# Longer runs for two weight loads, and the column order that goes with them

## The chip, the cores and the metric

The kernel runs on one core of a Trainium2 chip. The metric is the device time of one execution, in microseconds (us). The engines of a core work side by side, each from its own list of instructions: TensorE (PE; its weight loads are shown as PEld), VectorE (DVE), ScalarE (ACT), GpSimd (POOL) and SyncE (SP), which here does nothing but issue the transfers from device memory (DMAs). They wait for each other by semaphores.

## The reference, cut to what matters

One token per sequence, 8 sequences (B), model width 512 (D). First attention with 32 query heads over 8 key and value heads of a cache of which the last 2048 positions count, then a feed-forward block:

```python
x = A_x                                            # 8 x 512
h = x + A(_layernorm(x))                           # A: q = x@wq, softmax over 2048 keys, o, then o @ wo
u = _layernorm(h)                                  # what the block B gets
x1 = u + 0                                         # B's token shift is empty for one token, so w1, w2 add nothing
h2 = h + x1 + _gelu(_layernorm(x1) @ w3) @ w4      # w3: 512 x 1792, w4: 1792 x 512
```

All arrays are bf16. The keys and values that are read take 67 MB, wq and wo 4 MB each, w3 and w4 1.8 MB each.

## The kernel before, in words

**The stream.** SP issues all loads in one order written out by hand: wq, then 2 MB tiles of keys (`load_k`) and values (`load_v`) in turn, wo in three pieces (`load_wo`, heads 0 to 8, 8 to 24, 24 to 32 of each partition's 32 rows), then w3 (`load_w3`, 1792 KB) and w4 in three pieces (`load_w4`, 1024, 512 and 256 KB). All are recorded on one line, L207, in a helper `dma`, so they are told apart by the tile they write. The profile writes `w_sb` for both `w3_sb` and `w4_sb`. Each partition's share of a key tile is one run of 16 KB in device memory; w3 is loaded as four runs of 3584 bytes per partition (rows p, 128+p, 256+p, 384+p for partition p), w4's first piece (eight chunks of 128 rows) as two runs of four rows, 4096 bytes each.

**The attention** works through 64 tiles: PE turns a key tile (L383), ACT and DVE copy it out of PSUM (L393, L395), PE multiplies it with the queries (L408); softmax on DVE and ACT; then PE multiplies with the values (L504).

**The tail**, all on the last token of the chain and in this order on PE:

- `pe_x` (L565) starts the sum for h, kept with features on partitions: `hT_ps[:, nb*B:(nb+1)*B]` holds 128 features for 8 sequences, nb = 0 to 3. x is the stationary operand (the one that a weight load, LDWEIGHTS, puts into the array).
- `pe_wo_row` (L553) multiplies the first 20 of wo's 32 parts in row form, `pe_wo` (L574) the last 12 in column form: for each part and each nb, 128 columns of wo are loaded as the stationary operand and 8 columns of `oW` stream through. That makes 48 loads and 48 matmuls. `pe_hr` (L583, 8 loads) turns the row form over and adds it.
- mean, variance and normalisation: DVE L649 to L658, L689, L693, PE L652 and L683, ACT L692. `uT` (L654) is the normalised input of w3.
- `pe_w3` (L678): 14 column groups `fc`, 4 loads each of a 128 x 128 block of w3 as the stationary operand, 56 in all. Which columns belong to group fc is chosen by `w3_cols` so that the result lies as w4's rows do: with a run of k rows per partition, the columns are taken with a step of k. Before, W4_RUN is (4, 4, 4, 2): a step of four for groups 0 to 11, of two for 12 and 13.
- L703 on DVE scales, L705 on ACT applies gelu, in two halves, and L710 to L714 on DVE prepare the rest of the sum.
- `pe_w4` (L732): for each fc four matmuls side by side in four column strips of the array, each with `gT[:, fc, :]` stationary and 128 columns of w4 as the moving operand (the one that streams through). It comes in three calls, one for each piece of w4; `pe_fin` (L722) and a filler stand between the first two.
- L743 on ACT and L745 on DVE copy two strips each into `out_sb`, and SP stores it (L790).

Between these stand `warm_end(n)` calls (L493): n filler matmuls of 128x512 that nothing reads.

Of the kernel before, what the change touches and what calls it, by code (L numbers as in the profile page):

```python
# [11 lines left out]
B = 8  # L12
# [10 lines left out]
FC = F // 128  # L23
FG = FC // 2
KC = D // 128
# [54 lines left out]
def bass_sequential_preLN__sliding_block_cached__mixer_s_mlp__decode_kernel(  # L80
# [23 lines left out]
    with es:  # L104
# [13 lines left out]
        wo_v = wbig[:, :].rearrange("p (j n) -> p j n", j=JW)  # L118
        knat = sb([128, NK, CQ * DH], dt.bfloat16, "knat")
        vnat = sb([128, NV, CQ * DH], dt.bfloat16, "vnat")  # L120
        w3_sb = sb([128, KC, F], dt.bfloat16, "w3_sb")
        w4_sb = sb([128, FC, D], dt.bfloat16, "w4_sb")
# [13 lines left out]
        x_sb = sb([B, D], dt.bfloat16, "x_sb")  # L136
# [29 lines left out]
        sel32 = sb([128, H], dt.bfloat16, "sel32")  # L166

        orow = sb([128, 2, 512], dt.bfloat16, "orow")
        hr = orow
# [16 lines left out]
        out_sb = orow[0:B, 0, :]  # L186
# [13 lines left out]
        sem_x, sem_wq, sem_w3, sem_out = (S(n) for n in ("sem_x", "sem_wq", "sem_w3", "sem_out"))  # L200
        sem_wo = [S(f"sem_wo{i}") for i in range(len(WO_AT) - 1)]
        sem_w4 = [S(f"sem_w4{i}") for i in range(3)]
        PE, AC, DV, PO, SP = (Engine(S(n)) for n in ("s_pe", "s_act", "s_dve", "s_pool", "s_sp"))

        def dma(eng, dst, src, sem, *waits):
            def f(e):
                e.dma_start(dst, src).then_inc(sem, 16)  # L207
            eng.op(f, *waits, inc=False)
# [20 lines left out]
        e = DV.op(lambda e: e.bn_stats(st6[:, :], x_sb[:, :]), X)  # L229
        e = DV.op(lambda e: e.bn_aggr(mv[:, :], st6[:, :]), e)  # L230
        e = PO.op(lambda e: e.tensor_scalar(rstd[:, :], mv[:, 1:2], EPS, None, ALU.add), e)
        e = PO.op(lambda e: e.tensor_tensor(rstd[:, :], rstd[:, :], half[0:B, 0:1], ALU.pow), e)
# [8 lines left out]
        e = DV.op(lambda e: e.tensor_reduce(hsq[:, :], ident_f[:, :].rearrange("p (u h) -> p h u", u=4), AX.X, ALU.add))  # L241
# [7 lines left out]
        e = DV.op(lambda e: e.tensor_reduce(rows16[:, :].rearrange("p (t r) -> p t r", t=KQ),  # L249
                                            rows_f[:, :].rearrange("p (t s r) -> p t r s", t=KQ, s=NS), AX.X, ALU.add))  # L250
# [12 lines left out]
        e = PE.op(pe_xT, e_xln, e_idb)  # L263
# [67 lines left out]
        def q_turn():  # L331
            e_qT = []
            for j in range(2):
                def f(e, j=j):
                    for r in range(R):
                        ins = e.matmul(qT_ps[j][:, r * 128:(r + 1) * 128],
                                       qrow2[:, j, r, :, :].rearrange("p c d -> p (c d)").bitcast(dt.float32), ident_f[:, :],
                                       start=True, stop=True, is_transpose=True)
                    return ins
                e = PE.op(f, e_qrow[j], e_idf)  # L340
                got = qT_ps[j][:, :].bitcast(dt.bfloat16).rearrange("p (r u x) -> p r u x", r=R, u=4)[:, :, :, 0:2 * B]
                e_qT.append(DV.op(lambda e, j=j, got=got: e.tensor_copy(
                    qT[:, 4 * j:4 * (j + 1), :, :, :].rearrange("p u r b e -> p r u (b e)"), got), e))
            return e_qT[-1], e
# [145 lines left out]
        def warm_end(count):  # L490
            def f(e):
                for n in range(count):
                    ins = e.matmul(kbank[1], ident_b[:, :], still, start=True, stop=True)  # L493
                return ins
            PE.op(f, e_pT[LAST, 1])
# [49 lines left out]
        hT_ps = S_ps[0]  # L545
# [16 lines left out]
        def pe_x():  # L562
            def f(e):
                for nb in range(KC):
                    ins = e.matmul(hT_ps[:, nb * B:(nb + 1) * B], x_sb[:, nb * 128:(nb + 1) * 128],  # L565
                                   ident_b[0:B, 0:B], start=(nb == 0), stop=False, skip_group_check=True)
                return ins
            PE.op(f, free[0], X, e_idb)

        def pe_wo(j0, j1, piece):  # L570
            def f(e):
                for j in range(j0, j1):
                    for nb in range(KC):
                        ins = e.matmul(hT_ps[:, nb * B:(nb + 1) * B], wo_v[:, j, nb * 128:(nb + 1) * 128],  # L574
                                       oW[:, j, 0:B], start=False, stop=False, skip_group_check=True)
                return ins
            PE.op(f, (sem_wo[piece], 16))

        def pe_hr():
            def f(e):  # L580
                for part in range(2):
                    for nb in range(KC):
                        ins = e.matmul(hT_ps[:, nb * B:(nb + 1) * B], hr[:, part, nb * 128:(nb + 1) * 128], sel32[:, 0:B],  # L583
                                       start=False, stop=(part == 1), skip_group_check=True)
                return ins
            e_wo.append(PE.op(f, e_wo[-1], e_selb))
# [20 lines left out]
        e_qT, e_qturn = q_turn()  # L607
# [37 lines left out]
        def bc(a):  # L645
            return bass.AP(tensor=a.tensor, offset=a.offset, ap=[a.ap[0], [0, KC], [1, B]])


        e = DV.op(lambda e: e.tensor_reduce(hsum[:, :], vr(hT_ps[:, 0:NH]), AX.X, ALU.add), e_wo[-1])  # L649
# [11 lines left out]
        y_ps = [kbank[0], kbank[2]]  # L661
        FH = FC // 2

        W4_RUN = (4, 4, 4, 2)

        def w3_cols(kc, fc):
            at = 0
            for run in W4_RUN:
                if fc < at + run:
# [22 lines left out]
        e = AC.op(lambda e: e.activation(s2[:, :], vsum[:, :], ACT.Sqrt, bias=eps2[:, :], scale=1.0), e_vs)  # L692
        e_r2 = DV.op(lambda e: e.reciprocal(r2[:, :], s2[:, :]), e)  # L693

        def bcf(t):
            a = t[:, :]
            return bass.AP(tensor=a.tensor, offset=a.offset, ap=[a.ap[0], [0, FH], [1, B]])
# [3 lines left out]
        for n in range(2):  # L701
            cs = slice(n * FH * B, (n + 1) * FH * B)
            e = DV.op(lambda e, n=n, cs=cs: e.tensor_tensor(v3(g_x[:, cs]), v3(y_ps[n][:, 0:FH * B]), bcf(r2),  # L703
                                                            ALU.mult), e_y[n], e_r2)
# [3 lines left out]
        e = PO.op(lambda e: e.tensor_scalar(r1[:, :], vsum[:, :], EPS * (1.0 + EPS), None, ALU.add), e_vs)  # L708
        e = PO.op(lambda e: e.tensor_tensor(r1[:, :], r1[:, :], half[:, :], ALU.pow), e)
        e = DV.op(lambda e: e.tensor_tensor(v3(xb[:, :]), v3(hc[:, :]), bc(r1[:, :]), ALU.mult), e)  # L710
# [5 lines left out]
        z_ps = S_ps[1][:, 0:DH]  # L716

        def pe_fin():
            def f(e):
                for part in range(2):  # L720
                    for nb in range(KC):
                        ins = e.matmul(z_ps[32 * nb:32 * (nb + 1), :], fr[:, part, nb, :], ident_b[:, :],  # L722
                                       start=False, stop=False, tile_position=(0, 32 * nb), skip_group_check=True)
                return ins
            PE.op(f, e_fr)
        W4_AT = (0, 8, 12, FC)
        for n, waits in enumerate(((*e_gT, free[1]), (), ())):
            lo, hi = W4_AT[n:n + 2]
            def pe_w4(e, lo=lo, hi=hi):
                for fc in range(lo, hi):  # L730
                    for nb in range(KC):
                        ins = e.matmul(z_ps[32 * nb:32 * (nb + 1), :], gT[:, fc, :],  # L732
                                       w4_sb[:, fc, nb * 128:(nb + 1) * 128], start=(fc == 0), stop=(fc == FC - 1),
                                       tile_position=(0, 32 * nb), skip_group_check=True)
                return ins
            if n == 1:
                pe_fin()
                warm_end(1)
            e_z = PE.op(pe_w4, (sem_w4[n], 16), *waits)
        for nb in range(KC):  # L740
            to, got = out_sb[:, nb * 128:(nb + 1) * 128], z_ps[32 * nb:32 * nb + B, :]
            if nb % 2:
                e_outa = AC.op(lambda e, to=to, got=got: e.activation(to, got, ACT.Copy), e_z)  # L743
            else:
                e_outd = DV.op(lambda e, to=to, got=got: e.tensor_copy(to, got), e_z)  # L745
# [21 lines left out]
                            ap=[[KC * H * DH, k], [KC * k * H * DH, 4], [1, QF]]), sem_wf, e_wz if n else None)  # L767

        def load_w3():
            dma(SP, w3_sb[:, :, :], B_w3.rearrange("(k p) f -> p k f", p=128), sem_w3, e_qturn)  # L770

        def load_w4(n):
            lo, hi = W4_AT[n:n + 2]
            k = W4_RUN[-1] if hi == FC else W4_RUN[0]
            dma(SP, w4_sb[:, lo:hi, :].rearrange("p (g k) n -> p g (k n)", k=k),
                B_w4[lo * 128:hi * 128, :].rearrange("(g p k) n -> p g (k n)", p=128, k=k), sem_w4[n])

        turn = {"K": 0, "V": 0, "O": 0}
        for kind in "QKKK" + 9 * "VK" + "VKKVKVKVVVOVOO":
# [3 lines left out]
            {"K": load_k, "V": load_v, "O": load_wo}[kind](turn[kind])  # L783
            turn[kind] += 1
        load_w3()
        for n in range(3):
            load_w4(n)
# [39 lines left out]
```

## Time and profile before

| | us |
|---|---|
| median of 3 runs (192.92 to 194.08) | 193.04 |
| the profiled execution's own time | 193.02 |
| its span, first to last instruction | 191.6 |
| busy PE / PEld / DVE / ACT / POOL | 153.1 / 94.7 / 116.5 / 95.6 / 13.7 |

The span leaves out 1.42 us around the profiled execution, so a change in the span is added to 193.02. The page read 79.18 MB from device memory at a mean of 413 GB/s over the span; from the second slice of the page to the last but one the 16 DMA engines are busy without a gap. The granted TensorE clock is full (1.00) in all of the last 20 us. In the views, PE and PEld are two rows of one engine: loads run ahead of matmuls that are still streaming.

### The profile page before, as it was taken

How to read it: one execution, taken by the hardware profiler on the slowest of the kernel's cores; microseconds unless marked ns; L12 is line 12 of the kernel's file. 1: busy time of each engine (PE TensorE's matmuls, PEld its weight loads, DVE VectorE, ACT ScalarE, POOL GpSimd, SP SyncE). 2: the span in 40 equal slices, each digit the busy share in tenths (PEclk: the TensorE clock that was granted, in tenths of full speed). 3: DMA queues.
4: the chain of work that ended last, by engine and by line, in shares of the span. 5: the costliest groups of instructions: out<-in, count | busy, mean ns of one | idle time of the engine just before them, and what ended most of it. 6: DMA issues, size and time to landing. Idle time of an engine off the chain costs nothing.

```text
span 191.6 us, 3183 instructions
## 1 busy us (share of the span) xinstructions
PE 153.1 (80%) x1326; PEld 94.7 (49%) x1333; DVE 116.5 (61%) x259; ACT 95.6 (50%) x124; POOL 13.7 (7%) x37
## 2 busy tenths in 40 slices
PE   0049999598988988699978887889798895797895
PEld 0013866375556554465555455545554562343552
DVE  2733455834499368655885587558855886657423
ACT  3002667638357727284469255924782676340341
POOL 8400200100010001000100010002000000000040
PEclk9999999957999999789999999999999999699999
DMA  6999999999999999999999999999999999999991
GB/s 224 452 400 431 434 414 434 438 429 431 428 424 434 424 434 434 433 421 431 431 434 421 434 434 434 424 431 428 429 428 431 438 424 431 428 431 415 413 406 74
DMA packets 6477, 79.38 MB, mean 414 GB/s; under 512 B 688, under 2 KB 704, under 8 KB 1856
## 3 DMA queue, kind: packets, MB, share of 16 engines
q1 hardware_dynamic: 6448, 79.18, 97.3%
q8 instruction: 10, 0.16, 0.3%
q14 instruction: 3, 0.02, 0.0%
q10 hardware_dynamic: 16, 0.01, 0.0%
HBM read 79.18 MB, written 0.01 MB: 413 GB/s over the span
## 4 chain that ended last, share of the span: by engine, by line
DMA 55%; PE 20%; SPq 8%; DVE 8%; ACT 6%; issue 1%
DMA knat<-in_A_k_cache_dram 29%; DMA vnat<-in_A_v_cache_dram 11%; DMA w_sb<-in_B_w_dram 10%; SPq L207 8%; PE kT_ps L383 8%; DMA wbig<-in_A_wq_dram 6%; ACT kT_sb L393 3%; ACT pT_sb L472 3%; PE o_rows L504 3%; PE S_ps L504 3%; DVE kT_sb L395 2%; PE S_ps L302 2%; DVE oacc L516 2%; PE S_ps L408 2%; DVE omask L514 1%
## 5 line engine op out<-in xcount | busy, mean ns | idle before, releaser
L393 ACT ACTIVATE kT_sb<-kT_ps 128x1024 bf16<-128x1024 bf16 x64 | 65.6, 1025 | 54.9 <-PE kT_ps L383 54.7
L383 PE MATMUL kT_ps<-turn_f,knat 128*128 128x128 f32 x512 | 77.1, 291 | 13.8 <-DMA knat<-in_A_k_cache_dram 8.7
L383 PEld LDWEIGHTS kT_ps<-turn_f,knat 128*128 128x128 f32 x512 | 59.5, 147 | 35.0 <-issue 13.0
L395 DVE COPY kT_sb<-kT_ps 128x1024 bf16<-128x1024 bf16 x64 | 43.8, 685 | 25.4 <-PE kT_ps L383 25.2
L408 PE MATMUL S_ps<-kT_sb,qblk 128*32 128x512 bf16 x256 | 26.1, 401 | 2.7 <-ACT kT_sb L393 1.0
L504 PE MATMUL o_rows<-vnat,pT_sb 128*64 128x512 bf16 x128 | 16.5, 402 | 4.9 <-ACT pT_sb L472 4.9
L472 ACT ACTIVATE pT_sb<-o_rows,own_f 128x512 bf16<-128x512 f32 x28 | 17.7, 693 | 1.6 <-PE S_ps L408 1.2
L516 DVE TENSOR_REDUCE oacc<-omask 128x128 f32<-128x512 f32 x14 | 14.9, 1064 | 0.5
L504 PE MATMUL S_ps<-vnat,pT_sb 128*64 128x512 bf16 x112 | 13.4, 382 | 0.8 <-DMA vnat<-in_A_v_cache_dram 0.8
L504 PEld LDWEIGHTS o_rows<-vnat,pT_sb 128*64 128x64 bf16 x128 | 8.4, 114 | 11.3 <-issue 7.7
L350 POOL COPY qblk<-qT 64x64 bf16<-64x64 bf16 x16 | 5.0, 311 | 119.4 <-PE S_ps L408 106.4
L408 PEld LDWEIGHTS S_ps<-kT_sb,qblk 128*32 128x32 bf16 x256 | 6.6, 93 | 11.7 <-issue 6.9
L514 DVE TENSOR_TENSOR omask<-o_rows,own_s 128x512 f32<-128x512 f32 x7 | 4.8, 692 | 12.2 <-PE o_rows L504 12.2
L514 DVE TENSOR_TENSOR omask<-S_ps,own_s 128x512 f32<-128x512 f32 x7 | 4.8, 692 | 8.8 <-PE S_ps L504 8.8
L504 PEld LDWEIGHTS S_ps<-vnat,pT_sb 128*64 128x64 bf16 x112 | 5.8, 110 | 7.3 <-issue 2.0
L440 ACT ACTIVATE E_sb<-S_ps,negM 128x512 f32<-128x512 f32 x8 | 5.5, 689 | 6.5 <-DVE negM L436 6.5
L323 ACT ACTIVATE w_sb<-S_ps 128x512 bf16<-128x512 f32 x2 | 1.1, 594 | 11.4 <-PE S_ps L302 11.4
L259 PE MATMUL sm<-ident_b,xln_b 8*128 8x8 bf16 x4 | 0.3, 174 | 8.0 <-DVE xln_b L234 8.0
L529 PE MATMUL sm<-oacc,sel_o 128*128 128x256 f32 x16 | 6.1, 466 | 0.6 <-DVE oX L536 0.6
L431 DVE TENSOR_REDUCE mblk<-S_ps 128x1 f32<-128x512 f32 x8 | 5.5, 682 | 0.8 <-PE S_ps L408 0.8
L559 ACT ACTIVATE orow<-kT_ps 128x512 bf16<-128x512 f32 x1 | 0.6, 597 | 10.3 <-PE kT_ps L553 10.3
L453 DVE STREAM_TRANSPOSE PT_sb<-P_sb 128x512 bf16<-128x512 bf16 x8 | 5.6, 703 | 0.0
(118 smaller groups left out, 102.2 us busy)
## 6 DMA issues: line engine op xcount, KB each, us to landing
knat<-in_A_k_cache_dram SPq DMA_DIRECT2D x16, 2048.0 KB, 18.4
vnat<-in_A_v_cache_dram SPq DMA_DIRECT2D x15, 2048.0 KB, 20.1
wbig<-in_A_wq_dram SPq DMA_DIRECT2D x1, 3808.0 KB, 11.6
wbig<-in_A_wo_dram SPq DMA_DIRECT2D x2, 1024.0 KB, 22.5
knat<-in_A_v_cache_dram SPq DMA_DIRECT2D x1, 2048.0 KB, 19.8
wbig<-in_A_wo_dram SPq DMA_DIRECT2D x1, 2048.0 KB, 24.0
w_sb<-in_B_w_dram SPq DMA_DIRECT2D x1, 1792.0 KB, 29.9
w_sb<-in_B_w_dram SPq DMA_DIRECT2D x1, 1024.0 KB, 31.9
```

The lines of the kernel that those rows point to most:

```text
L207: e.dma_start(dst, src).then_inc(sem, 16)
L383: ins = e.matmul(kT_ps[i % 2][:, n * 256:(n + 1) * 256].bitcast(dt.float32), knat[:, j % NK, c * DH:(c + 2) * DH].bitcast(dt.float32), tur ...
L393: e_lo[i] = AC.op(lambda e: e.activation(kT_sb[:, i % NKT, 0:W // 2], kT_ps[i % 2][:, 0:W // 2], ACT.Copy), e_Tlo[i], e_QK.get(i - NKT))
L395: e_hi[i] = DV.op(lambda e: e.tensor_copy(kT_sb[:, i % NKT, W // 2:W], kT_ps[i % 2][:, W // 2:W]), e_Thi[i], e_QK.get(i - NKT))
L408: ins = e.matmul(S_ps[b % 2][32 * t:32 * (t + 1), :], qblk[:, b % 2, KQ * q + t, half, at:at + H], kT[:, :, t, :, half], start=(q == 0 and ...
L431: e = DV.op(lambda e: e.tensor_reduce(mblk[:, 0:1], S_ps[b % 2][:, :], AX.X, ALU.max), e_QK[G * b + G - 1], e_mz)
L453: e_PT[b] = DV.op(lambda e: e.transpose(PT_sb[:, :], P_sb[:, :]), e_P[b], e_wide.get(b - 1))
L472: e_pT[b, t] = AC.op(lambda e: e.activation(pT_sb[:, b % 2, :, H * t:H * (t + 1)], bank[:, :].rearrange("p (n y) -> p n y", n=NN), ACT.Cop ...
L504: ins = e.matmul(bank[64 * u:64 * (u + 1), :], pT_sb[:, b % 2, n, :].rearrange("p (x q) -> p q x", q=NQ)[:, q, :], v_tile(m)[:, n * 512:(n ...
L514: free[at] = DV.op(lambda e: e.tensor_tensor(omask[:, :, :], bank.rearrange("p (s d) -> p s d", s=NS), own, ALU.mult), e_PV[m], e_acc.get( ...
L516: e_acc[m] = DV.op(lambda e: e.tensor_reduce(acc, omask[:, :, :].rearrange("p s d -> p d s"), AX.X, ALU.add), free[at], e_O.get(b - 2))
L529: e_O[b] = PE.op(lambda e: e.matmul(O_ps, sel_o[:, :], oacc[:, b % 2, :, :].rearrange("p q d -> p (q d)"), start=True, stop=True), e_acc[N ...
```

## The change

Three edits that belong together. w3's rows are laid on the partitions in another order: partition p now gets rows 4p to 4p+3, one run of 14,336 bytes. The features of the normalised input must lie in the same order, so whatever writes them takes every fourth column, starting from nb, instead of a block of 128: x in `pe_x`, wo in `pe_wo`, the turned rows in `pe_hr`. Because the rest of the sum (`fin`) has the same order, w4's output columns and the place in `out_sb` get the step of four too. And w4's first piece is loaded with eight rows (8192 bytes) in one run, which makes `w3_cols` step by eight for groups 0 to 7; groups 8 to 11 keep four, 12 and 13 two.

```diff
         def pe_x():
-                    ins = e.matmul(hT_ps[:, nb * B:(nb + 1) * B], x_sb[:, nb * 128:(nb + 1) * 128],
+                    ins = e.matmul(hT_ps[:, nb * B:(nb + 1) * B], x_sb[:, nb::KC],
...
         def pe_wo(j0, j1, piece):
-                        ins = e.matmul(hT_ps[:, nb * B:(nb + 1) * B], wo_v[:, j, nb * 128:(nb + 1) * 128],
+                        ins = e.matmul(hT_ps[:, nb * B:(nb + 1) * B], wo_v[:, j, nb::KC],
...
         def pe_hr():
-                        ins = e.matmul(hT_ps[:, nb * B:(nb + 1) * B], hr[:, part, nb * 128:(nb + 1) * 128], sel32[:, 0:B],
+                        ins = e.matmul(hT_ps[:, nb * B:(nb + 1) * B], hr[:, part, nb::KC], sel32[:, 0:B],
...
-        W4_RUN = (4, 4, 4, 2)
+        W4_RUN = (8, 4, 2)
...
             def pe_w4(e, lo=lo, hi=hi):
-                                       w4_sb[:, fc, nb * 128:(nb + 1) * 128], start=(fc == 0), stop=(fc == FC - 1),
+                                       w4_sb[:, fc, nb::KC], start=(fc == 0), stop=(fc == FC - 1),
...
         for nb in range(KC):
-            to, got = out_sb[:, nb * 128:(nb + 1) * 128], z_ps[32 * nb:32 * nb + B, :]
+            to, got = out_sb[:, nb::KC], z_ps[32 * nb:32 * nb + B, :]
...
         def load_w3():
-            dma(SP, w3_sb[:, :, :], B_w3.rearrange("(k p) f -> p k f", p=128), sem_w3, e_qturn)
+            dma(SP, w3_sb[:, :, :].rearrange("p k f -> p (k f)"), B_w3.rearrange("(p k) f -> p (k f)", k=KC), sem_w3, e_qturn)

         def load_w4(n):
-            k = W4_RUN[-1] if hi == FC else W4_RUN[0]
+            k = W4_RUN[n]
```

The number and the order of instructions on every engine stay the same; on SP two of the 39 entries have another shape, w3's load and the first of w4's.

## The prediction

> **What bounds the kernel now.** I began with the page's strip of 40 slices: the DMA row stands at 9 from the second slice to the last but one, so the stream of loads sets the pace until close to the end. Then I read the end of the chain of work that ended last (start, duration, what):
>
> ```profile
> 170.00 19.17 DMA w_sb<-in_B_w_dram
> 189.17 0.04 issue
> 189.22 0.32 PE S_ps L732 x8
> ...
> 189.88 0.28 DVE orow L745
> ```
>
> The last thing waited for is w4's third piece, landed at 189.17; the last 8 matmuls, the copies and the store follow. To gain, that landing must come earlier; to lose, PE must become later than it. How close is PE? The timeline of the tail, PE's rows (start, duration, what, in brackets the idle time before):
>
> ```profile
> 180.15 1.27 PEld L574 LDWEIGHTS S_ps<-oW,wbig 128*128 128x128 bf16 x48 [0.42 <-issue]
> ...
> 181.65 0.27 PEld L583 LDWEIGHTS S_ps<-sel,orow 128*128 128x128 bf16 x8 [0.23 <-DVE orow L560]
> ...
> 183.53 1.24 PE L493 MATMUL kT_ps<-ident_f,ident_b 128*128 128x512 bf16 x5
> ...
> 184.93 1.87 PEld L678 LDWEIGHTS kT_ps<-uT,w_sb 128*128 128x128 bf16 x56 [0.65 <-DMA w_sb<-in_B_w_dram]
> ...
> 186.76 1.02 PE L493 MATMUL kT_ps<-ident_f,ident_b 128*128 128x512 bf16 x4
> ...
> 187.71 0.63 PE L732 MATMUL S_ps<-w_sb,qrow 128*32 128x128 bf16 x32
> ...
> 188.70 0.23 PEld L732 LDWEIGHTS S_ps<-w_sb,qrow 128*32 128x32 bf16 x16 [0.23 <-DMA w_sb<-in_B_w_dram]
> ...
> 189.22 0.12 PEld L732 LDWEIGHTS S_ps<-w_sb,qrow 128*32 128x32 bf16 x8 [0.28 <-DMA w_sb<-in_B_w_dram]
> ```
>
> Here the reader sees a tail in which PE waits little. w3's pass starts 0.04 us after w3's landing (184.89, the issue at 155.01 plus 29.9), but w4's first pass does not wait for its transfer (landed 187.34): the fillers L493 start 0.216 us apart, so the fourth streams until 187.62, and the next load starts 0.09 later. The same holds at 188.70 (landing 188.58). Only the last two groups, at 189.22, truly wait. Without that wait they would start 4 groups x 0.056 after 188.70, at 188.93: PE has **0.29 us** in hand there, and no more.
>
> **The transfers.** The view by stretches (PE, PEld, DVE, ACT, POOL busy, clock, DMA share, GB/s) prices the runs:
>
> ```profile
> 140.00:160.00 20.00, 17.96 (x148) 11.23 (x147) 13.50 (x28) 11.85 (x15) 0.00 (x0) 1.00 1.01 431
> 182.00:184.00 2.00, 1.79 (x11) 0.82 (x10) 0.96 (x6) 0.21 (x2) 0.00 (x0) 1.00 1.02 416
> ```
>
> With 16 KB runs 431 GB/s, in w3's stretch with 3.5 KB runs 416. The trace's packet records say the same more finely: on one engine's ring, packets of 3584, 4096, 8192 and 16,384 bytes start 136.5, 155.5, 306 and 607 ns apart, some 5 ns per packet beside the bytes. A 14,336-byte packet is then 607 - 2048 x 301/8192 = 532 ns against 4 x 136.5 = 546, 14 ns less per partition. Each of 16 engines serves 8 partitions: 0.11 us off w3. w4's first piece: 2 x 155.5 - 306 = 5 ns, times 8, 0.04 us. Together **0.15 us** earlier for the last landing. By the packets' recorded durations (140, 159, 309, 611 ns) it is 0.20 + 0.07 = **0.27 us**. I keep both ends. SP issues fewer descriptors; its last issue ended long before (174.2), so that is worth nothing. No load before w3 is touched.
>
> **The weight loads with a step of four** (L565, L574, L583). This row exists in the trace: w3's groups 0 to 11 are loaded so today. The starts of single loads are 33.3 ns apart there, 25.0 in groups 12 and 13 (step two) and 25.0 in L574 and L583 (no step). So each load of a 128x128 block gets 8.3 ns dearer. L565: 4 of them, finished a microsecond before L553 gets its last `oW`, hidden. L574: 48 x 8.3 = 0.40 us; L583 follows 0.28 after the last matmul's slot ends, since it waits for DVE L560, so 0.12 shows, and L583 adds 8 x 8.3 = 0.07. Everything up to `warm_end(5)` moves by about 0.18 us: the fillers stop at 184.79 instead of 184.61. w3's landing moves to 184.69 to 184.78. So w3's pass starts near 184.80, **0.13 us earlier** than today, now held by PE.
>
> **The weight loads with a step of eight** (32 of the 56 in L678). No row shows them. Lower end: as dear as a step of four, 33.3 ns, if each column is fetched by itself from that step on. Upper end of the plain cases: double, 66.7 ns, if the cost goes with the bytes passed over. Steps of two and four lie at 25.0 (perhaps a floor, as no step is 25.0 too) and 33.3, and a line through these two gives 50. I take 58, the middle of 50 and 67, as the nearest rows rise with the step. Price: 32 x (58 - 33.3) = **0.79 us** on w3's pass.
>
> [...]
>
> **w4's moving columns with a step of four** (L732). The nearest row with a step is L408, which streams keys with a step of two: its 512 columns last 391 ns, against 390 for the first unstepped ones in L553. So lower end nothing, which I take; upper end double, as no moving row has a step of four: 0.056 us per group more, 14 groups, 0.78 us. A gain has no mechanism: 128 columns stream either way.
>
> **The copies into `out_sb`.** DVE L245 writes 128 columns of bf16 with a step of four in 300 ns, the L745 copies take 282: at most 0.02 each, 0.04 in all. ACT has no stepped row; the nearest, L705, writes blocks of 8 in 249 ns. I take nothing; if ACT's two doubled it would be 0.5 us.
>
> **The sum.** With a step-of-eight load at s ns, PE's last two groups are ready so: w3's pass ends at 186.76 - 0.13 + 32 x (s - 33.3)/1000; four fillers 0.86; 0.09 to the first load of w4; then as in the trace 0.46 for eight groups, 0.22 for L722, 0.32 for a filler, 0.28 to the last group's start. Together 188.85 + 32 x (s - 33.3)/1000, against 189.28 today. The gelu half (L703, L705) moves with w3's end and stays under the fillers, as it does now (gelu done 187.44, fillers 187.62). With s = 58: 189.64, **0.36 us later**. With s = 50, 0.10; with 67, 0.64. From s = 47 on PE is later than today's end; below about 40 the landing decides. The profiled execution had 193.02, the median is 193.04, so no correction: **193.4 us**. All this is under 1%, which is about what a measurement of this kernel tells from no change (its three runs spread over 0.6%).
>
> **The rivals.**
>
> - *The step of eight costs no more than four.* Then PE is at 188.85 and the landing, 0.15 to 0.27 earlier, sets the end: 192.75 to 192.87. For: no step and a step of two cost the same, so cost doesn't simply follow the step. Against: two to four is a rise.
> - *The moving step of four costs too.* With double streaming and s = 58, 14 groups add 0.78: 194.2; with s from 50 to 67, 193.9 to 194.4. With s = 33 it is PE at 189.63, 193.4. For: a moving operand asks for a column every 0.4 ns, so it is the more sensitive one. Against: L408's step of two is free.
> - *The slower one: step-of-eight loads stall in full.* It decides from +1.93 us, 32 x (s - 33.3) = 2.36 us, s = 107 ns. At four times today's 33.3, s = 133, PE's end comes at 192.04: 195.8 us, 1.4% slower. For: such a load has only been seen to get dearer with the step. Against: the rise from two to four is 8 ns.
> - *The change doesn't do what it says*: the 14 KB runs are cut up again into smaller packets. Then w3 lands when it did; PE's price stays, and the time is the forecast's, 193.4. Against: key tiles go as single packets of 16 KB, wq's rows as packets of 30,464 bytes.
> - *Much faster*: the whole tail would have to shrink by 1.93 us, and only 0.15 to 0.27 of the stream goes away. I see no row for it.
>
> **How the numbers follow.** Chances: forecast 0.45; step of eight free 0.25; moving step dear 0.12; full stall 0.08; packets cut 0.04; faster by over 1% 0.02; other mishaps 0.04, half of them slow. From these, faster 0.02, slower 0.10, within 1% 0.88. The range goes from the earliest landing, 192.75 with 0.05 for scatter, to the dear moving step, 194.4: 192.7 to 194.4. It holds the first three cases and the fifth, 0.86; leaving out the moving step would leave 0.74.
>
> **What would show it.** Right: 128 packets of 14,336 bytes some 532 ns apart; the loads of L574 33 ns apart; those of L678 50 to 67 ns apart in groups 0 to 7 and w3's pass near 2.6 us long instead of 1.87; no DMA wait before the last groups of L732; groups of L732 still 56 ns apart. Wrong: groups of L678 at 33 ns and a DMA wait left at the end (then 192.8); groups of L732 over 100 ns apart; L743 or L745 over 320 ns; or a w3 landing that hasn't moved.

## The result and the profile after

The changed kernel takes **195.3 us** (median of 6 runs, 195.07 to 196.44) against 192.98 for the kernel before: a ratio of 1.0116, with a 95% interval from 1.0072 to 1.016. It is slower by about 2.3 us, and outside the range of the prediction. The profiled execution took 195.07 us with a span of 193.7, against 193.02 and 191.6. Of both kernels two runs of six lie more than a microsecond above the other four (194.08 and 194.46 before, 196.30 and 196.44 after).

The end of the chain of waits of the changed kernel (start, duration, what):

```profile
184.93 2.82 PE kT_ps L678 x56
187.75 0.97 PE kT_ps L493 x4
188.73 1.03 PE S_ps L732 x31
189.76 0.21 PE S_ps L722 x8
189.97 0.54 PE kT_ps L493
190.51 0.82 PE S_ps L732 x24
191.34 0.02 issue
191.36 0.44 ACT orow L743
```

From w3's landing on no transfer is in it any more: PE runs through, and the copies end it. The timeline of the same stretch:

```profile
179.98 1.68 PEld L574 LDWEIGHTS S_ps<-oW,wbig 128*128 128x128 bf16 x48 [0.42 <-issue]
...
184.93 2.74 PEld L678 LDWEIGHTS kT_ps<-uT,w_sb 128*128 128x128 bf16 x56 [0.65 <-DMA w_sb<-in_B_w_dram]
...
187.61 1.11 PE L493 MATMUL kT_ps<-ident_f,ident_b 128*128 128x512 bf16 x4
...
188.66 1.10 PE L732 MATMUL S_ps<-w_sb,qrow 128*32 128x128 bf16 x32
...
189.91 0.61 PE L493 MATMUL kT_ps<-ident_f,ident_b 128*128 128x512 bf16 x1
...
190.44 0.87 PE L732 MATMUL S_ps<-w_sb,qrow 128*32 128x128 bf16 x24
191.36 0.90 DVE L745 CAST orow<-S_ps 8x128 bf16<-8x128 f32 x2 [2.58 <-PE S_ps L732]
191.36 0.92 ACT L743 ACTIVATE orow<-S_ps 8x128 bf16<-8x128 f32 x2 [3.07 <-PE S_ps L732]
```

Set against the lines of before, step by step: w3's pass starts at the same time and lasts 2.68 us to the first filler instead of 1.82 (+0.86). From there to w4's first load it takes 1.04 instead of 0.95 (+0.09). w4's first eight groups last 0.91 instead of 0.46 (+0.45), L722 and the single filler 0.88 instead of 0.54 (+0.34), the rest of w4 with its latency 0.92 instead of 0.86 (+0.06; before, 0.28 of it was the wait for the last piece). The copies last 0.92 instead of 0.60 (+0.32). Together 2.1 us, which is the difference of the spans. The lines of before for the filler and the copies:

```profile
188.39 0.39 PE L493 MATMUL kT_ps<-ident_f,ident_b 128*128 128x512 bf16 x1
...
189.56 0.56 ACT L743 ACTIVATE orow<-S_ps 8x128 bf16<-8x128 f32 x2 [2.13 <-PE S_ps L732]
189.56 0.60 DVE L745 CAST orow<-S_ps 8x128 bf16<-8x128 f32 x2 [1.65 <-PE S_ps L732]
```

Two things in these lines were not foreseen: w4's groups are 115 ns apart instead of 56, and the single filler lasts 0.61 instead of 0.39. The view by stretches of the changed kernel says what the second is (the number before the DMA share is the granted TensorE clock):

```profile
core 0: us, PE busy (x) PEld busy (x) DVE busy (x) ACT busy (x) POOL busy (x), PEclk, DMA share, GB/s
185.00:188.40 3.40, 3.40 (x60) 2.90 (x60) 0.76 (x5) 1.06 (x3) 1.02 (x1) 1.00 0.67 268
188.40:191.80 3.40, 2.91 (x67) 1.74 (x65) 0.78 (x3) 0.44 (x1) 0.00 (x0) 0.50 0.01 3
```

The clock is halved from 188.42 to 191.83, in the middle of w4. In the profile of before it is whole there (the same two stretches, 1.00 and 1.00).

### The profile page after: what moved, and what is told of

Read it like the earlier page. It is cut to its first block, busy times and chain, and to the rows that moved or that the text cites. A ratio compares the mean times of both kernels' runs of the same rounds, so it can differ in the third digit from the quotient of the medians.

```text
span 193.7 us, 3183 instructions
## 1 busy us (share of the span) xinstructions
PE 156.8 (81%) x1326; PEld 97.7 (50%) x1333; DVE 116.8 (60%) x259; ACT 96.0 (50%) x124; POOL 13.7 (7%) x37
## 4 chain that ended last, share of the span: by engine, by line
DMA 60%; PE 23%; DVE 7%; ACT 7%; issue 1%; SPq 1%
DMA knat<-in_A_k_cache_dram 29%; DMA w_sb<-in_B_w_dram 16%; DMA vnat<-in_A_v_cache_dram 10%; PE kT_ps L383 8%; DMA wbig<-in_A_wq_dram 6%; ACT pT_sb L472 4%; PE o_rows L504 3%; PE S_ps L504 3%; ACT kT_sb L393 2%; DVE kT_sb L395 2%; PE S_ps L302 2%; DVE oacc L516 2%; PE kT_ps L678 1%; PE S_ps L408 1%; PE sm L529 1%; DVE omask L514 1%
## 5 line engine op out<-in xcount | busy, mean ns | idle before, releaser
L383 PEld LDWEIGHTS kT_ps<-turn_f,knat 128*128 128x128 f32 x512 | 60.1, 148 | 33.3 <-issue 13.0
L408 PE MATMUL S_ps<-kT_sb,qblk 128*32 128x512 bf16 x256 | 26.4, 404 | 2.3 <-ACT kT_sb L393 0.6
L408 PEld LDWEIGHTS S_ps<-kT_sb,qblk 128*32 128x32 bf16 x256 | 6.6, 93 | 11.8 <-issue 8.1
L529 PE MATMUL sm<-oacc,sel_o 128*128 128x256 f32 x16 | 7.1, 530 | 0.6 <-DVE oX L536 0.6
```

The costliest lines, as they stand in the source:

```text
L383: ins = e.matmul(kT_ps[i % 2][:, n * 256:(n + 1) * 256].bitcast(dt.float32), knat[:, j % NK, c * DH:(c + 2) * DH].bitcast(dt.float32), tur ...
L408: ins = e.matmul(S_ps[b % 2][32 * t:32 * (t + 1), :], qblk[:, b % 2, KQ * q + t, half, at:at + H], kT[:, :, t, :, half], start=(q == 0 and ...
L529: e_O[b] = PE.op(lambda e: e.matmul(O_ps, sel_o[:, :], oacc[:, b % 2, :, :].rearrange("p q d -> p (q d)"), start=True, stop=True), e_acc[N ...
```

## The experiments

The first four asked which of the three stepped accesses costs what, and whether the clock falls on their account. My theory then: three costs, the loads with a step of eight, the copies, and the clock, which the longer pass brings down. The rival: w4's moving columns cost by themselves.

**w4's first piece back in runs of four rows.** On the changed kernel:

```diff
-        W4_RUN = (8, 4, 2)
+        W4_RUN = (4, 4, 4, 2)
```

> The changed kernel with w4's first piece back in runs of four rows, so that no weight load of w3 has a step of eight; w3 in 14 KB runs and all steps of four stay. Theory (three costs: loads with a step of eight at 60 ns, a halved TensorE clock that follows from the longer pass, copies with a step of four): w3's pass is 1.82 us again instead of 2.68, the clock stays whole to the end, groups of L732 are 56 ns apart, and only the copies' 0.32 us stay: 193.1 to 193.5 us. Rival (the moving step of four makes L732's groups 115 ns by itself, whatever the clock): groups of 115 ns at full clock, 193.6 to 194.0. Rival (the clock falls for another reason than the long pass): clock halved near 188.4, 194.3 or more.

Measured: 194.25 us (193.63 to 195.0), ratio 1.0056 (1.0034 to 1.0078). w3's pass is back at 1.83 us. In the profiled execution (195.00) the clock was halved from 182.87 to 186.29, so up to the start of w3's pass, and whole from there on. w4's part of it shows the rival right:

```profile
188.92 1.11 PE L732 MATMUL S_ps<-w_sb,qrow 128*32 128x128 bf16 x32
```

and in the view by stretches, of L732 alone:

```profile
core 0: us, PE busy (x) PEld busy (x), PEclk, DMA share, GB/s
188.95:189.75 0.80, 0.80 (x32) 0.79 (x32) 1.00 0.00 0
```

Eight groups take as long as in the changed kernel, 115 ns each, at a clock of 1.00, where a group took 56 before the change. So the step of four in the moving operand costs by itself, and the part of my theory that put this on the clock falls. The time is another matter: the median lies above the 193.6 to 194.0 that this rival gave. The theory and this rival had the clock whole, and the other rival had it halved near 188.4; that it falls before w3's pass nobody expected.

**Only w4's first piece changed.** On the kernel before:

```diff
-        W4_RUN = (4, 4, 4, 2)
+        W4_RUN = (8, 4, 2)
...
-            k = W4_RUN[-1] if hi == FC else W4_RUN[0]
+            k = W4_RUN[n]
```

> The kernel before with one edit, w4's first piece in 8 KB runs: w3's columns of groups 0 to 7 have a step of eight, nothing else is stepped anew (no step in wo, w4's columns, copies). Theory (the long pass brings the clock down): w3's pass 2.68 us, clock halved from about 188.4, groups of L732 107 ns apart, copies 0.6 us: 194.6 to 195.1 us. Rival (the clock fell because of wo's or w4's stepped reads): clock whole, groups of 56 ns, 193.4 to 193.8.

Measured: 194.46 us, ratio 1.0069 (1.0039 to 1.0098), and both sides had a part of it: of ten runs four took 193.34 to 193.48 and six 194.40 to 195.98. w3's pass lasted 2.70 us in the profiled execution (194.40), and its clock was halved from 189.01 on. The other nine runs have no trace, but each run's mean granted clock is on record: 0.964 to 0.973 in the four lower ones, 0.937 to 0.956 in the six upper ones. So the longer pass alone costs some 0.5 us (against 192.97), and a fallen clock, going by these means, in some runs 1.0 to 2.5 more.

**w4's columns in blocks again**, on the changed kernel:

```diff
-                                       w4_sb[:, fc, nb::KC], start=(fc == 0), stop=(fc == FC - 1),
+                                       w4_sb[:, fc, nb * 128:(nb + 1) * 128], start=(fc == 0), stop=(fc == FC - 1),
```

> The changed kernel with w4's moving columns in blocks of 128 again (the output's columns then come out in another order than the reference's). Theory: the clock is still halved, groups of L732 at 107 ns instead of 115, about 0.1 us less than the changed kernel: 195.1 to 195.3. Rival (the moving step is what costs): groups of 56 ns, 0.8 us or more less, 194.5 or below.

Measured: 195.83 us (195.36 to 196.27), above what either side gave. In the profiled execution (195.36) the clock was halved from 187.88 to 191.30, so already under the four fillers before w4, which took 1.60 us instead of the changed kernel's 1.04; why the other three runs gained nothing, no trace shows. The durations speak:

```profile
187.65 1.67 PE L493 MATMUL kT_ps<-ident_f,ident_b 128*128 128x512 bf16 x4
...
189.25 1.04 PE L732 MATMUL S_ps<-w_sb,qrow 128*32 128x128 bf16 x32
...
190.98 0.65 PE L732 MATMUL S_ps<-w_sb,qrow 128*32 128x128 bf16 x24
```

Groups start 107 ns apart while the clock is half, and 56 ns apart after it came back, between the last three groups. Here unstepped columns followed the clock; stepped ones took 115 ns a group at 0.50 (the changed kernel) as at 1.00 (w4's first piece in runs of four rows).

**The copies in blocks again**, on the changed kernel:

```diff
-            to, got = out_sb[:, nb::KC], z_ps[32 * nb:32 * nb + B, :]
+            to, got = out_sb[:, nb * 128:(nb + 1) * 128], z_ps[32 * nb:32 * nb + B, :]
```

> The changed kernel with the copies into out_sb in blocks of 128 columns again (the output's columns then come out in another order than the reference's). Theory: L743 and L745 take 0.27 to 0.28 us each instead of 0.44, the two pairs 0.60 instead of 0.92, all else as in the changed kernel: 0.32 us less, 194.9 to 195.1. Rival (the copies are slow since PSUM or the engines are slower in that state): 0.44 stays, 195.3.

Measured: the pairs of copies last 0.56 (ACT) and 0.59 us (DVE), as before the change; the time, 195.94 (195.78 to 196.73), is not lower, where 194.9 to 195.1 was expected. In the profiled execution the clock was halved twice in the tail, from 182.94 to 186.35 and from 189.76 to 193.17. Times of kernels whose clock falls in different places can't be compared to 0.3 us, so what the copies cost is read from their durations alone, and the next experiments went for the clock.

**What brings the clock down.** In the traces the clock changes on a grid of 3.41 us: between two changes lie 3.41 us or a whole multiple of it (in the changed kernel's trace 3.41, 17.07, 20.48, 34.13 and 44.37, which is 1, 5, 6, 10 and 13 times). Its place differs from run to run (a fall at 188.42 there, at 182.87 with w4's first piece in runs of four rows, at 189.01 with that piece alone changed). Counting each matmul of the tail with its columns (0.42 ns each at the whole clock, as the fillers' 512 columns start 0.216 us apart) and overlaps once, I worked out for each window of the grid the share in which columns stream, and what the clock was in the next window. In the tails of the kernels so far: shares of 0.40 to 0.55 were followed by a whole clock, shares of 0.13, 0.25, 0.29, 0.30, 0.34, 0.34 and 0.39 by a halved one. PE's busy time was no guide: the window before the fall in the changed kernel shows 3.40 of 3.40 us busy above, and 0.29 of streaming, since a weight load of 60 ns is followed by 8 columns, some 3 ns. If that is the cause, more columns under the same loads must keep the clock.

On the second kernel above (w4's first piece alone), w3's pass streams its 8 input columns eight times (what reads the result takes one copy of the eight):

```diff
-                        ins = e.matmul(y_ps[n][:, f * B:(f + 1) * B],
+                        a = uT[:, kc * B:(kc + 1) * B]
+                        eight = bass.AP(tensor=a.tensor, offset=a.offset, ap=[a.ap[0], [0, 8], [1, B]])
+                        ins = e.matmul(y_ps[n][:, f * 64:(f + 1) * 64],
                                        w3_cols(kc, fc),
-                                       uT[:, kc * B:(kc + 1) * B], start=(kc == 0), stop=(kc == KC - 1))
+                                       eight, start=(kc == 0), stop=(kc == KC - 1))
```

> The kernel before with w4's first piece in 8 KB runs, as in b_eight, and in w3's pass each matmul streams the 8 columns of the input eight times over (64 columns, 56 of them not used). Theory (the clock is halved after a 3.4 us window in which too few columns stream, under some 0.40 of the window in the traces so far; with the 60 ns loads w3's pass brings that window down to 0.14 to 0.39): 64 columns take 27 ns and hide under a load of 60, the share rises by about 0.3, the clock stays whole after w3's pass, the loads stay 60 ns apart, and nearly all runs are at b_eight's lower cluster, 193.3 to 193.7. Rival (the clock follows something else, as the number of matmuls or of loads): still over half of the runs at 194.4 or more, median near 194.5.

Measured: 193.59 us (193.46 to 194.21, 11 runs), ratio 1.001 (0.9982 to 1.0037). No run is at 194.4 or above, where six of ten were. The stretches of the pass and of w4, of the kernel without and then with the 64 columns:

```profile
185.60:189.00 3.40, 3.40 (x78) 2.74 (x81) 1.10 (x6) 0.50 (x2) 0.40 (x1) 1.00 0.57 228
189.00:192.40 3.40, 1.98 (x57) 1.08 (x45) 0.56 (x2) 0.54 (x2) 0.00 (x0) 0.50 0.00 0
```

```profile
185.00:188.40 3.40, 3.27 (x60) 3.02 (x60) 0.53 (x4) 1.14 (x3) 1.25 (x1) 1.00 0.70 283
188.40:191.80 3.40, 1.92 (x68) 1.01 (x65) 1.13 (x5) 0.69 (x3) 0.00 (x0) 1.00 0.02 9
```

w3's pass is no shorter (2.72 us in its profile against 2.70 without the wide matmuls), and the clock stays.

**The copies, and the lines they write.** On the changed kernel, ACT copies in blocks to a place that is not stored, DVE with the step:

```diff
+            to = out_sb[:, nb * 128:(nb + 1) * 128] if nb % 2 else out_sb[:, nb::KC]
-            to, got = out_sb[:, nb::KC], z_ps[32 * nb:32 * nb + B, :]
+            to, got = (orow[0:B, 1, (nb // 2) * 128:(nb // 2 + 1) * 128] if nb % 2 else to), z_ps[32 * nb:32 * nb + B, :]
```

> The changed kernel with ACT's two copies in blocks and into another place, DVE's two still with a step of four (half of the output's columns are left out). Theory (a step of four in an 8 x 128 copy out of PSUM costs by itself): L745 on DVE 0.44 us each, L743 on ACT 0.27. Rival (ACT and DVE hinder each other since they write into the same lines): both at 0.27 to 0.29.

The timeline (the edit moves these lines down by one):

```profile
190.99 0.56 ACT L744 ACTIVATE orow<-S_ps 8x128 bf16<-8x128 f32 x2 [2.68 <-PE S_ps L732]
190.99 0.89 DVE L746 CAST orow<-S_ps 8x128 bf16<-8x128 f32 x2 [2.20 <-PE S_ps L732]
```

The step itself costs: DVE's two copies take 0.43 us each, as in the changed kernel, and 0.28 in blocks. The rival is out: with ACT elsewhere DVE is as slow as before. This execution happened to keep the clock whole to the end and took 194.67 us, with w4's groups 115 ns apart.

**w4's strips on different rows.** On the changed kernel, the four strips of a group read four different rows of w4:

```diff
-                                       w4_sb[:, fc, nb::KC], start=(fc == 0), stop=(fc == FC - 1),
+                                       w4_sb[:, lo + (fc - lo + nb) % (hi - lo), nb::KC], start=(fc == 0), stop=(fc == FC - 1),
```

> The changed kernel, but the four strips of a group of L732 read four different rows of w4 each, still with a step of four (so the sums are not the reference's); no two strips read the same bytes' neighbourhood at a time. Theory (the step itself halves the rate at which a moving operand is read): groups stay 115 ns apart. Rival (the four strips ask for the same lines at once): groups of 56 ns at whole clock, 107 at half.

Measured in one run (196.30 us, clock halved from 188.91): groups 116 ns apart in w4's first call. In its second call the clock comes back at 192.32, after which no group starts, so this run shows 116 at the half clock alone, where the rival expected 107. The step costs with the strips apart too. That four strips read at once stays part of this price: no run streams a stepped operand alone.

**What is left without the steps.** w3 in its long run, w4's first piece in runs of four rows, and the order undone in `pe_fin`, so that w4's columns and the copies are in blocks. On the first kernel of this section, with the columns of L732 and the copies as they were before the change:

```diff
                     for nb in range(KC):
-                        ins = e.matmul(z_ps[32 * nb:32 * (nb + 1), :], fr[:, part, nb, :], ident_b[:, :],
-                                       start=False, stop=False, tile_position=(0, 32 * nb), skip_group_check=True)
+                        for s in range(KC):
+                            ins = e.matmul(z_ps[32 * s:32 * (s + 1), nb::KC], fr[:, part, nb, :],
+                                           ident_b[:, 32 * s:32 * (s + 1)],
+                                           start=False, stop=False, tile_position=(0, 32 * s), skip_group_check=True)
```

> w3 in 14 KB runs with wo's, x's and hr's steps of four, w4's first piece in runs of four rows, and the order undone in pe_fin: 32 matmuls of 32 columns, written into PSUM with a step of four, instead of 8 of 128, so that w4's columns and the copies are in blocks. Theory (the change without its three dear parts): groups of L732 at 56 ns, copies 0.28, pe_fin 0.2 to 0.4 us instead of 0.22 and partly hidden in the wait for the last piece: 192.8 to 193.2 at whole clock, no measurable difference from before. Rival (longer runs are worth the 0.15 to 0.27 us predicted): 192.7 to 192.85 with the last wait for a transfer still there. Rival (the stepped PSUM writes are slow): 193.4 or more.

Measured: 193.01 us (192.64 to 194.82, 12 runs), ratio 1.0004 (0.9968 to 1.0039). Its timeline (the edit moves lines down by two):

```profile
187.70 0.63 PE L734 MATMUL S_ps<-w_sb,qrow 128*32 128x128 bf16 x32
...
188.84 0.65 PE L734 MATMUL S_ps<-w_sb,qrow 128*32 128x128 bf16 x24
...
189.54 0.59 DVE L747 CAST orow<-S_ps 8x128 bf16<-8x128 f32 x2 [1.64 <-PE S_ps L734]
```

The first and the last stand where they stood before the change (187.71, 189.56). The second call of w4 starts 0.14 us later than the 188.70 of before, since `pe_fin` now takes longer, and the wait for the last piece takes that up. The longer run of w3 is worth nothing in time that can be told. The four runs over 194 have mean granted clocks of 0.938 to 0.947, the seven under 193.2 have 0.964 to 0.973, so the clock was lower in these four too; where it fell in them, no trace shows.

**All three kernels with the clock held.** Each matmul of L574 and of w3's pass streams 32 columns: of `oW` its 24 empty columns too, of the normalised input four copies. On the kernel before, on the changed one and on the one just shown; the core of the edit, with the readers of the two results following it:

```diff
-                        ins = e.matmul(hT_ps[:, nb * B:(nb + 1) * B], wo_v[:, j, nb * 128:(nb + 1) * 128],
-                                       oW[:, j, 0:B], start=False, stop=False, skip_group_check=True)
+                        ins = e.matmul(hT_ps[:, nb * 32:(nb + 1) * 32], wo_v[:, j, nb * 128:(nb + 1) * 128],
+                                       oW[:, j, :], start=False, stop=False, skip_group_check=True)
...
-                        ins = e.matmul(y_ps[n][:, f * B:(f + 1) * B],
+                        a = uT[:, kc * B:(kc + 1) * B]
+                        four = bass.AP(tensor=a.tensor, offset=a.offset, ap=[a.ap[0], [0, 4], [1, B]])
+                        ins = e.matmul(y_ps[n][:, f * 32:(f + 1) * 32],
                                        w3_cols(kc, fc),
-                                       uT[:, kc * B:(kc + 1) * B], start=(kc == 0), stop=(kc == KC - 1))
+                                       four, start=(kc == 0), stop=(kc == KC - 1))
```

> The kernel before, all loads and orders as they were, but each matmul of L574 and of w3's pass streams 32 columns instead of 8 (of oW its 24 empty columns too, of the normalised input four copies; 24 of 32 result columns are not read). Theory (the clock is halved after a window with under some 0.39 of streamed columns): by the trace of before only windows that begin between 179.2 and 180.7 us fall under it, 0.27 at the lowest, and the 32 columns lift these to about 0.45, so the runs at 193.6 to 195.2 that the kernel before has now and then (8 of 23 in the last comparison) go away, and all are at 192.7 to 193.4. Rival (these runs have another cause): as often as before.

> The changed kernel with the same 32 columns in L574 and in w3's pass. Theory: with the clock whole the three stepped accesses alone are left, w3's pass 0.86 longer, L732's groups at 115 ns, copies 0.32 longer: 194.5 to 194.9 in nearly all runs, no run over 195.2, against 195.07 to 196.44 for the changed kernel. Rival (the steps cost this much without the clock): 195.3 as in the changed kernel.

> fin_order (w3 in 14 KB runs, w4 in runs of four rows, order undone in pe_fin) with the same 32 columns. Theory: runs at 192.6 to 192.95 only, none over 193.5; against the kernel before at 192.97 a gain of 0.1 to 0.3 us, under what can be told. Rival (longer runs are worth nothing): 192.9 to 193.2.

| kernel | as it is: median (range) | with 32 columns: median (range, 12 runs), ratio to the kernel before |
|---|---|---|
| before | 192.99 (192.70 to 194.58, 29 runs) | 192.89 (192.71 to 193.16), 0.998 (0.996 to 1.000) |
| changed | 195.30 (195.07 to 196.44, 6 runs) | 194.50 (194.34 to 195.61), 1.0061 (1.0035 to 1.0087) |
| order undone in `pe_fin` | 193.01 (192.64 to 194.82, 12 runs) | 192.85 (192.66 to 193.63), 0.9979 (0.9958 to 1.0001) |

The theory holds in the main, with one run outside it in two of the three: 195.61 of the changed kernel, where none was to be over 195.2, and 193.63 of the last, where none was to be over 193.5. Of the kernel before, 7 of 29 runs in the same comparison were at 193.6 or above, of the one with 32 columns none. The changed kernel loses all upper runs but one, and 0.8 us by the medians. What then remains of its loss, 1.5 us by the medians, is the steps: in its profile w3's pass is as long as ever and w4's groups are 115 ns apart at the whole clock (the edit moves lines down by three):

```profile
184.58 2.73 PEld L681 LDWEIGHTS kT_ps<-uT,w_sb 128*128 128x128 bf16 x56 [0.42 <-DMA w_sb<-in_B_w_dram]
...
188.21 1.12 PE L735 MATMUL S_ps<-w_sb,qrow 128*32 128x128 bf16 x32
...
190.66 0.92 ACT L746 ACTIVATE orow<-S_ps 8x128 bf16<-8x128 f32 x2 [2.71 <-PE S_ps L735]
```

and by stretches, of w4's groups alone (PE and PEld busy, clock, DMA share, GB/s):

```profile
188.25:189.00 0.75, 0.75 (x28) 0.75 (x32) 1.00 0.02 8
```

The last kernel is the best of all by its median, but its interval reaches 1: no version is shown to beat the kernel before.

## Why the prediction was wrong, by its own steps

**Right.** The weight loads with a step of four: L574's are 33.3 ns apart. The loads with a step of eight, taken at 58: they are **60.0 ns** apart, and w3's pass has 0.86 more where 0.79 was forecast. The last wait for a transfer is gone, as PE had only 0.29 us in hand. The packets: 128 of 14,336 bytes, eight of them 4257 ns on an undisturbed engine, 532 each.

**Wrong: "w4's moving columns with a step of four".** I took the lower end, nothing, by the row of L408, whose step is two. The upper end was the truth: 115 ns a group against 56, 14 groups, 0.83 us where the bound said 0.78. Here the step of two (391 ns for 512 columns, against 390 for the first unstepped ones in L553) did not show what the step of four costs; and the weight loads had just shown that between these two the cost begins (25.0, 25.0, 33.3 ns for no step, two and four). I weighed that against a rival's chance of 0.12 instead of taking it as the nearest row.

**Wrong: "the copies into `out_sb`".** Taken at nothing. The end of the copies moved by 0.32 us: ACT's pair takes 0.92 instead of 0.56, DVE's 0.90 instead of 0.60. The row I leaned on, DVE L245, reads SBUF and writes 128 partitions; L745 reads PSUM, and its 0.28 became 0.44. Which of these differences makes the price was not tried.

**Left out: the clock.** The text took it as given, since it was 1.00 over the last 20 us. It isn't given: in this tail and by my count, windows of 3.41 us with a streaming share up to 0.39 were followed by a halved one, three windows apart (they stand in the last section), and the pass made longer by 60 ns loads is such a place (0.29 in the changed kernel). By the trace of before, windows that begin between about 179.2 and 180.7 us (share down to 0.27) are under 0.40, and barely a few others (0.37 to 0.39, as those from 182.9 to 183.5); by the trace of the changed kernel also those from 182.8 to 185.8 (down to 0.17). With windows of 3.41 us, hardly any place of the grid is left that avoids both. That costs 0.8 us by the medians with and without the 32 columns, and shows in the profile of the changed kernel as L722 and the single filler at 0.50: 0.88 us together instead of 0.54.

**Right in the packets, little of it at the end: the 0.15 to 0.27 us.** In the two profiles compared, the last landing was only 0.02 us earlier (189.15 against 189.17). In both executions one engine lost some 0.47 us within w3: after the change one packet took 1000 ns instead of 535, before it two in a row took 388 and 362 instead of 140. So this delay does not tell the two apart. In the traces of all thirteen kernels, one of each, it lies within w3 in the four with the short runs, which have their last landing at 189.17 to 189.35, and in four of the nine with 14 KB runs, which have it at 189.15 to 189.18. In the other five it comes before w3, and the last landing at 188.79 to 189.02. Like with like that is some 0.1 us, and how much of the 0.15 to 0.27 arrives stays open. It doesn't matter: with PE late, nothing waits for it.

**Wrong, though without weight: w3's pass "0.13 us earlier", "now held by PE".** In the profile after the change it started at 184.93 as before, held by w3's landing (184.88). From the start of L574 to L652 it takes 2.31 us instead of 2.14, so the 0.18 forecast for the loads with a step of four is about right, but L574 began 0.17 us earlier in that execution (179.98 against 180.15).

The sum, with the two terms that I set to nothing put at what was bounded or measured: 193.4 + 0.78 + 0.32 = 194.5, the median of the changed kernel with its clock held. That it fits so closely is in part luck, as the start of w3's pass, put at 184.80, was 184.93 in one profile and 184.58 in the other. The rest up to 195.3 is the clock.

## What to carry to other kernels

A step in an operand of TensorE was a price per instruction here, and it has to be read from a row with that step: two was free (25.0 ns a weight load, as without a step; 391 ns for 512 moving columns, against 390 for the first unstepped ones in L553), four cost a third more as a weight load (33.3 ns) and double as moving columns (115 ns a group against 56, four strips side by side), eight 2.4 times a plain load (60.0 ns). A saving on transfers of a quarter of a microsecond was not worth such steps in a tail where PE has 0.29 us in hand: with the clock held they left 1.5 us of loss. In the window before the clock fell PE was busy 3.40 of 3.40 us, and columns streamed for 0.29 of it by my count; so in a tail of weight loads with few columns behind them it is worth counting the columns that stream, not only the busy time.

## What the runs showed that I had not expected

- The clock followed streamed columns in this tail, with exceptions: in the tails of all thirteen traces, by my count, windows of 3.41 us with a share up to 0.39 were followed by a halved clock and windows from 0.40 by a whole one. Three windows with 0.31, 0.36 and 0.38, followed by a whole clock, stand against that. They are those in which w4's columns stream with their step; counted with the 115 ns that a group takes, they have 0.44, 0.54 and 0.44. The number is not one to carry elsewhere: between 20 and 150 us of the same executions, 23 of 28 windows with 0.40 to 0.46 were followed by a halved clock. A window with PE busy throughout can be followed by a halved one (3.40 of 3.40 us busy before the fall in the changed kernel). The exact share, and whether the array counts columns or something that goes with them, stays open.
- Idle columns held it cheaply here: 24 empty columns of `oW` and three copies of the input cost nothing under the loads (192.89 us by the median, against 192.99), and with them no run of the kernel before was at 193.6 us or above (12 runs within 192.71 to 193.16, against 7 of 29).
- Moving columns with a step of four, in four strips side by side, took 115 ns per 128, with the clock at 1.00 (w4's first piece in runs of four rows; the changed kernel with 32 columns) as at 0.50 (the changed kernel), so what limited them here wasn't the array's clock.
